# Taking two chunks through one half of the feed-forward features, then the other, in the first batch

## The chip, the cores and the metric

The kernel runs on one core of one Trainium2 chip. The metric is device time in microseconds (us) of one execution. A core has five engines with a queue of their own each: TensorE (PE) for matrix products, VectorE (DVE), ScalarE (ACT) and GpSimd (POOL) for elementwise work, and SyncE (SP), which here only issues transfers (DMA). They wait for one another by semaphores.

## The reference

```python
x: (8, 3008, 256) float32
X = np.fft.fft(np.fft.fft(x, axis=1), axis=2).real     # FNet mixing
x = X.reshape(8 * 3008, 256)
gate = 1 / (1 + np.exp(-(x @ w_gate)))                 # w_gate, w_val: (256, 1536)
out = (gate * (x @ w_val)) @ w_out                     # w_out: (1536, 256)
```

The three weights come as float64, and the kernel decodes them to float32 itself.

## The kernel before, in words

**Mixing.** A batch is folded by its symmetries (`fold_ops`), and its transform along the sequence is a set of matrix products with tables of cosines and sines (`seq_group`, `half`). Their results are evacuated by `places` into rows `pk` (cosines), `qk` (sines) and `ek` (the features' Nyquist row) of 1506 elements. For batch 0 the cosine products come first, in two halves as x arrives, then the sine products; `load_table` loads the tables.

**Weights.** The transform along the features is not done on x but on the weights: `merge` multiplies a gate or value weight block by a small table on TensorE (tile name `ps`), and ScalarE copies the result to `G1` and `G2`; two small transfers spread G2's first row to `ge`. A weight goes through the engines as a job: `weight_load` (a 512 KB transfer on SP), `weight_parts` (two ScalarE steps, L259 and L260), `weight_join` (three VectorE steps, L269, L270 and L272, then one on GpSimd, L274), and `weight_use`, which is the merge for gate and value blocks. `jobs` is the list of the 18 jobs, six blocks each of gate, value and output weights. An output weight block feeds `forms`: 11 sums (L315) and four ScalarE copies for each group of three feature tiles, in two parts, on GpSimd for groups 0 and 1 and on VectorE for 2 and 3.

**Feed-forward.** 1505 positions (mirrored, they make all 3008) are cut into six chunks of up to 252. The 1536 features are 12 tiles of 128, and the main loop has one iteration i for each batch, chunk and feature tile: 8 x 6 x 12 = 576. In an iteration TensorE does

- `front_a(i)`: two products with `pk` (gate and value), into a PSUM bank of `pf`
- a merge, where `use` holds one for this iteration
- `back`: a third (five products, tile names `po0` to `po4`) of the output products of the group of three feature tiles that ended two iterations earlier
- `front_b(i)`: two products with `qk`, onto the same bank of `pf`

Between them a copy `ae` of the bank is taken (on VectorE by L521 for i below 12, with the term of `ek` added; from 12 on by ScalarE, L518, on a bank that ScalarE has seeded with that term, L504). `gate_a(i-1)` and `gate_b(i-1)` then make both halves of h: VectorE forms z and two products, ScalarE two sigmoids, and GpSimd adds up the sums `sf` (L560) that the output products need (a bilinear scheme with 15 products in place of more). Then come the iteration's jobs: `pre` holds the rounds of parts and join, `use` the uses, and `parts_` the waiting parts of `forms`.

The output products of a chunk accumulate over its four groups in five PSUM banks. In the last group each bank is evacuated to a tile `c` (L584, ScalarE and VectorE in turn); `finish` puts the chunk's 20 sums of `c`, its transposes and its stores on the list `later`, from which each iteration takes two or three.

**Order.** All queues are strictly in the order in which the program is written (`manual_schedule`); nothing is rescheduled. Pools give buffers in turn: three PSUM banks for `pf` and `ps`, five for `po`; two tiles `c`; one `os`, which is `ek` of batch 0 before it serves for the stores. The staging of jobs 0 to 9 borrows tiles that the loop uses later (`home`), that of the later ones borrows the tile of x (three places for raw data), so they are loaded once the sine products of batch 0 have read x. The lines that place the jobs are

```python
for then, js in zip(evacuate, ((2, 3, 4), (5,), (), (), (6, 7), (8,))):
    weight_round(*js)
    then()()
```

that is, the rounds of jobs 2 to 8 between the six evacuations of batch 0's transform, and, in the loop, the round of job j (from 9) at iteration j - 9; the merges of block c at iterations 2c - 3 (gate) and 2c - 2 (value).

Of the kernel before, what the change touches and what calls it, by code (L numbers as in the profile page):

```python
# [75 lines left out]
def kernel(  # L76
# [122 lines left out]

    jobs = [(w, c - (w == 2)) for c in range(NPR + 1) for w in range(3)
            if (c if w == 2 else c < NPR)]
    RAW, WS = {}, {}
    shared = {}
    KEEP = 10
# [94 lines left out]
    def forms(g):  # L301

        w = [WO[f // 2].rearrange("p f (a h j) -> p f h a j", h=2, j=TB)[:, f % 2]
             for f in range(3 * g, 3 * g + 3)]
        f = wf[:, g].rearrange("p m (a j) -> p m a j", j=TB)
        engine = nc.gpsimd if g < 2 else nc.vector

        def block(i):
            return w[i // 2][:, i % 2] if i < 6 else f[:, i - 6]

        def some(lo, hi):
            for i, (a, sign) in enumerate(W_COPIES if lo == 0 else ()):
                nc.scalar.mul(f[:, len(W_SUMS) + i], block(a), float(sign))
            for i, (a, b, op) in list(enumerate(W_SUMS))[lo:hi]:
                engine.tensor_tensor(f[:, i], block(a), block(b), op=(ALU.subtract, ALU.add)[op])  # L315
        return [lambda lo=lo: some(lo, lo + 6) for lo in range(0, len(W_SUMS), 6)]
# [160 lines left out]

    chunks = [(k0, min(CH, -(-(NK - k0) // 3) * 3)) for k0 in range(0, NK, CH)]
    assert NK <= chunks[-1][0] + chunks[-1][1] <= NK + 1 and NFT == 12
    groups = [(b, c, g) for b in range(B) for c in range(len(chunks)) for g in range(NG)]  # L480
    H, SF, EK = {}, {}, {}

    def cut(i):
        b, c, _ = groups[i // 3]
        k0, n = chunks[c]
        f = i % NFT
        return PQE[b], slice(k0, k0 + n), n, f, slice(f * P, (f + 1) * P)

    def e_rows(i):

        b, c, _ = groups[i // 3]
        k0, n = chunks[c]
        EK[i // NFT] = ekp.tile([P, CH], F32, name="ek", tag="ek")[:, 0:n]
        nc.sync.dma_start(out=EK[i // NFT], in_=ed[b : b + 1, k0 : k0 + n].to_broadcast([P, n]))

    PF, AP, Z = {}, {}, {}

    def seed(i):


        _, _, n, f, _ = cut(i)
        PF[i] = bank("pf").rearrange("p (g n) -> p g n", g=2)[:, :, 0:n]
        for g in range(2 if i >= NFT else 0):
            nc.scalar.activation(PF[i][:, g], EK[i // NFT], AF.Copy, scale=ge[:, g, f : f + 1])  # L504

    def front_a(i):
        (pk, *_), ks, _, _, fs = cut(i)
# [59 lines left out]
    def back(p, part):  # L567

        b, c, g = groups[p]
        n = chunks[c][1]  # L570
        R = 2 * n // 3
        last = p == len(groups) - 1
        if part == 0 and g == 0:
            PO[:] = [pso.tile([P, 2 * WC], F32, name=f"po{t}", tag=f"po{t}") for t in range(NB)]
        for at_, (hb, wb) in list(enumerate(PRODUCTS))[part * 5 : part * 5 + 5]:
            t, j = divmod(PLACE[at_], 3)
            mm(PO[t][:, j * R : (j + 1) * R], wf[:, g, wb], block(p, hb), g == 0 and at_ % 3 == 0,
               g == NG - 1)
            if g == NG - 1 and at_ % 3 == 2:
                if t == 0:  # L580
                    C[0] = cp.tile([P, 10 * WC], F32, name="c", tag="c")
                    nc.gpsimd.memset(C[0][:, 15 * R : 15 * R + 40], 0.0)
                if not (last and t == NB - 1):
                    (nc.vector.tensor_copy if t % 2 else nc.scalar.copy)(  # L584
                        C[0][:, 3 * t * R : 3 * (t + 1) * R], PO[t][:, 0 : 3 * R])
        if part == 2:
            del H[p], SF[p]
            if g == NG - 1:
                finish(b, c, last)

    def finish(b, c, last):
        k0, n = chunks[c]
        R = 2 * n // 3
        more = k0 + n > NK
        nb = -(-n // TB)
        t = C.pop(0)
# [12 lines left out]

        def flip(s, h):  # L610
            if not os_:
                os_.append(op.tile([P, NK + 1], F32, name="os", tag="os")[:, 0 : 4 * WC].rearrange(
                    "p (s b h j) -> p s b h j", s=2, h=2, j=TB))
            c0 = OUT[h] * R + (n + more if s else 0)
            nc.vector.transpose(os_[0][:, s, 0:nb, h, :], t[:, c0 : c0 + nb * TB])

        def store(s):
            m, r0 = (min(n, M - k0), b * S + k0) if s == 0 else (
                n - (k0 == 0) - more, b * S + S - k0 - n + 1 + more)
            full = m // TB  # L620
            for a in range(4):
                ps = slice(a * TB, (a + 1) * TB)
                cs = slice(a * 2 * TB, (a + 1) * 2 * TB)
                queues[a % len(queues)].dma_start(
                    out=out[r0 : r0 + full * TB, cs].rearrange("(b t) d -> t b d", t=TB),
                    in_=os_[0][ps, s, 0:full].rearrange("p b h j -> p b (h j)"))
                if m > full * TB:
                    queues[a % len(queues)].dma_start(out=out[r0 + full * TB : r0 + m, cs],
                                      in_=os_[0][a * TB : a * TB + m - full * TB, s, full].rearrange(
                                          "p h j -> p (h j)"))  # L630

        def add(f):
# [21 lines left out]
        weight_load(j)  # L654
    load_x(0)
    load_table(0, NQ // 2)
    for j in range(2, 6):
        weight_load(j)
    load_table(1, NQ)
    for j in range(6, KEEP):  # L660
        weight_load(j)

    def weight_round(*js):
# [18 lines left out]
    for sums, _, _ in sin:  # L682
        sums(*range(NQ))
    evacuate = [then for _, then, _ in cos + sin]
    for then, js in zip(evacuate, ((2, 3, 4), (5,), (), (), (6, 7), (8,))):
        weight_round(*js)
        then()()
    nc.scalar.dma_start(out=ed[0:1], in_=PQE[0][2][0:1])
    nc.vector.tensor_copy(PQE[0][1][0:1, 0:CH], PQE[0][2][0:1, 0:CH])
    for j in range(KEEP, KEEP + 3):  # L690
        weight_load(j)
    weight_use(2)
# [4 lines left out]
    def at(i, *fs):  # L697
        side.setdefault(i, []).extend(fs)

    pre, use = {}, {}
    for j in range(9, len(jobs)):
        pre.setdefault(j - 9, []).append(lambda j=j: weight_round(j))
        if KEEP <= j < len(jobs) - 3:
            at(j - 9, lambda j=j: weight_load(j + 3))
    for j in range(3, len(jobs)):
        w, c = jobs[j]
        i = (0, 1, 4, 7, 9, 10)[c] if w == 2 else 2 * c - 3 + w
        use.setdefault(i, []).append(lambda j=j: weight_use(j))  # L710


# [2 lines left out]
    calm = lambda lo: (i for i in range(lo, count) if 3 <= i % i0 <= 7)  # L715
    for i, f in enumerate(mirror_x(1)):
        at(i0 - 3 + i // 2, f)
    at(i0 + 2, lambda: load_x(1))
    for b in range(1, B):
        at(i0 + 2 + b, lambda b=b: e_load(b))  # L720
    for i, f in enumerate(mirror_tables()):
# [1 line left out]
    at(3 * i0, e_fold)  # L723
    at(3 * i0 + 4, lambda: e_sums()())
    at(3 * i0 + 6, table_again)
    for i in range(i0, count, i0):
        at(i - 8, lambda i=i: e_rows(i))

    for b in range(B - 1):
# [1 line left out]
        g0 = s0 + 3 * i0 + 4 if b else 5 * i0 + 4  # L731


        slots = [i for i in range(s0 - 2 * i0 if b > 1 else s0 if b else 2 * i0, g0) if i % i0 < 4]

        def folds(slots, b=b):
            ops = fold_ops(b + 1, 2)
# [11 lines left out]
    for i in range(count):  # L749
        front_a(i)  # L750
        if i < NFT:
            part(i)
        if i:
            gate_a(i - 1)
        if i >= NFT:
            part(i)
        if i0 <= i + 1 < count:
            seed(i + 1)
        if i:
            gate_b(i - 1)  # L760
        todo = pre.pop(i, []) + use.pop(i, [])
        for f in [parts_.pop(0)] + todo if parts_ else todo + [lambda: parts_ and parts_.pop(0)()]:
            f()
        if i >= 5:
            back((i - 5) // 3, (i - 5) % 3)
        front_b(i)
        for f in later[0 : 2 + i % 2]:
            f()
        del later[0 : 2 + i % 2]
        for f in side.pop(i, []):  # L770
            f()
    gate_a(count - 1)
# [54 lines left out]
```

## Time and profile before

| what | value |
|---|---|
| median of 3 runs | 1982.71 us (1982.51 to 1985.28) |
| the profiled execution | 1985.11 us, its span 1983.2 us |
| TensorE busy | 1936.4 us, 98% of the span |
| VectorE, ScalarE, GpSimd busy | 1488.3, 1338.3, 1624.8 us |
| TensorE busy from 0 to 50 us | 32.70 us |
| TensorE busy from 50 to 130 us | 68.25 us |
| TensorE busy from 200 to 1900 us | 1696.71 us |
| first line of the loop on TensorE, second product of i = 0 | starts at 54.77 us |

All times in the profile count from the start of the span; the execution's own time is 1.9 us longer than the span. A row of the timeline gives the start, the length, the engine, the line, the operation, and the tiles written and read; in brackets stands how long the engine had been idle before it and what it waited for. Several instructions of one kind in a row are drawn together (xN). Two TensorE instructions in a row make one product here, so a product of `pf` for gate and value shows as x4, a merge as x8 and a third of the output products as x10. Lines named L127 are all TensorE's, since one helper issues every product.

### The profile page before, as it was taken

To read this page: it belongs to the slowest core of one execution; us is meant where nothing else is said; L and a number is where in the kernel's file an instruction comes from. 1 tells how busy PE (TensorE), PEld (TensorE's weight loads), DVE (VectorE), ACT (ScalarE), POOL (GpSimd) and SP (SyncE) were. 2 spreads that over 40 slices of the span, in tenths; PEclk is the share of its full clock that TensorE was granted. 3 is DMA by queue.
4 is the path that set the end of the run, shared out by engine and by line. 5 is a ranking of instruction groups with operands and counts; after the bars stand their busy time and mean duration, and the time that the engine had idled before them with its cause. 6 is when DMAs were issued, how large, how long until landed. Compare 5 with 4: busy or idle time off the path is not lost.

```text
span 1983.2 us, 34391 instructions
## 1 busy us (share of the span) xinstructions
PE 1936.4 (98%) x11232; PEld 1790.2 (90%) x11232; DVE 1488.3 (75%) x3179; ACT 1338.3 (67%) x3102; POOL 1624.8 (82%) x2857
## 2 busy tenths in 40 slices
PE   6899999999999999999999999999999999999997
PEld 4689889998999899998999989999899989999996
DVE  7788777886787677786778867787678777777776
ACT  3467667675777667775777757777577766777774
POOL 3879898997889878997889868998688886777775
PEclk8999999999999999999999999999999999999999
DMA  8353423212112120222013121221210110011001
GB/s 266 88 132 85 124 50 104 51 22 78 18 46 54 19 77 14 54 50 77 15 21 78 20 77 20 45 54 20 77 22 14 18 23 14 14 18 23 14 16 30
DMA packets 171444, 101.41 MB, mean 51 GB/s; under 512 B 133890, under 2 KB 163204, under 8 KB 168588
## 3 DMA queue, kind: packets, MB, share of 16 engines
q1 hardware_dynamic: 169294, 98.64, 20.3%
q8 instruction: 90, 1.47, 0.3%
q10 hardware_dynamic: 1940, 0.56, 0.1%
q14 instruction: 88, 0.72, 0.1%
q0 software_dynamic: 32, 0.00, 0.0%
HBM read 74.45 MB, written 50.18 MB: 63 GB/s over the span
## 4 chain that ended last, share of the span: by engine, by line
PE 94%; DMA 2%; DVE 2%; POOL 1%; ACT 1%; issue 0%; SPq 0%; ACTq 0%; DVEq 0%; POOLq 0%
PE pf L127 48%; PE po L127 41%; PE ev L127 4%; DMA ge<-G 1%; DMA st<-in_stab_dram 1%; PE od L127 1%; PE ps L127 0%; DVE wf L315 0%; DMA wx<-in_moe_w_val_dram 0%; DVE ae L521 0%; POOL sf L560 0%; POOL wf L315 0%; DVE z L539 0%; DMA raw<-in_moe_w_gate_dram 0%; DMA wx<-in_moe_w_gate_dram 0%
## 5 line engine op out<-in xcount | busy, mean ns | idle before, releaser
L560 POOL TENSOR_TENSOR sf<-h 128x168 f32<-128x168 f32 (+1 forms) x960 | 550.8, 592 | 233.1 <-DVE h L556 233.0
L560 POOL TENSOR_TENSOR sf<-h,sf 128x168 f32<-128x168 f32 (+1 forms) x1152 | 646.1, 581 | 54.2 <-DVE h L556 54.2
L127 PE MATMUL pf<-qk,G 128*128 128x252 f32 (+1 forms) x2304 | 582.7, 376 | 3.8 <-DVE ae L521 1.9
L127 PE MATMUL pf<-pk,G 128*128 128x252 f32 (+1 forms) x2304 | 583.0, 376 | 0.0
L556 DVE TENSOR_TENSOR h<-z 128x252 f32<-128x252 f32 (+1 forms) x576 | 293.7, 510 | 377.0 <-ACT z L555 376.4
L504 ACT ACTIVATE pf<-ek,ge 128x252 f32<-128x252 f32 (+1 forms) x1128 | 531.4, 471 | 18.4
L127 PE MATMUL po<-sf,wf 128*128 128x168 f32 (+1 forms) x3072 | 530.4, 306 | 0.0
L518 ACT ACTIVATE ae<-pf 128x504 f32<-128x504 f32 (+1 forms) x564 | 332.6, 590 | 240.1 <-PE pf L127 239.3
L127 PEld LDWEIGHTS pf<-pk,G 128*128 128x128 f32 x2304 | 436.3, 190 | 53.1 <-issue 2.3
L127 PEld LDWEIGHTS po<-sf,wf 128*128 128x128 f32 x3072 | 473.3, 190 | 8.4
L127 PE MATMUL po<-h,wf 128*128 128x168 f32 (+1 forms) x2688 | 475.9, 306 | 2.1 <-ACT a L471 1.6
L607 DVE TENSOR_TENSOR c<-c 128x168 f32<-128x168 f32 (+1 forms) x950 | 467.1, 514 | 8.5
L127 PEld LDWEIGHTS po<-h,wf 128*128 128x128 f32 x2688 | 427.5, 190 | 19.2 <-ACT a L471 2.0
L127 PEld LDWEIGHTS pf<-qk,G 128*128 128x128 f32 x2304 | 409.9, 190 | 30.7 <-DVE ae L521 2.9
L542 DVE TENSOR_TENSOR z<-ae,pf 128x504 f32<-128x504 f32 (+1 forms) x564 | 372.4, 660 | 19.1 <-ACT h L537 18.8
L537 ACT ACTIVATE h<-pf 128x252 f32<-128x252 f32 (+1 forms) x576 | 218.7, 380 | 172.3 <-PE pf L127 160.2
L555 ACT ACTIVATE z<-z 128x252 f32<-128x252 f32 (+1 forms) x576 | 230.8, 401 | 76.7 <-DVE z L542 46.5
L554 DVE TENSOR_TENSOR h<-h,pf 128x252 f32<-128x252 f32 (+1 forms) x576 | 231.7, 402 | 0.0
L560 POOL TENSOR_TENSOR sf<-sf 128x168 f32<-128x168 f32 (+1 forms) x192 | 114.3, 595 | 15.1
L127 PE MATMUL ev<-st,x 63*128 63x376 f32 (+4 forms) x372 | 99.0, 418 | 8.8 <-DVE x L338 6.0
L560 POOL TENSOR_TENSOR sf<-sf,h 128x168 f32<-128x168 f32 (+1 forms) x192 | 107.5, 560 | 0.0
L127 PEld LDWEIGHTS ev<-st,x 63*128 63x128 f32 (+1 forms) x372 | 66.8, 188 | 37.0 <-issue 7.3
(115 smaller groups left out, 876.5 us busy)
## 6 DMA issues: line engine op xcount, KB each, us to landing
x<-xr SPq DMA_DIRECT2D x14, 1536.0 KB
out_dram<-os SPq DMA_DIRECT2D x380, 56.0 KB
xr<-in_xf_dram SPq DMA_DIRECT2D x14, 768.0 KB
xr<-in_xf_dram SPq DMA_DIRECT2D x35, 256.0 KB
ek<-ed SPq DMA_DIRECT2D x39, 126.0 KB
out_dram<-os SPq DMA_DIRECT2D x288, 7.0 KB
x<-in_xf_dram SPq DMA_DIRECT2D x2, 1512.0 KB
tr<-in_stab_dram SPq DMA_DIRECT2D x2, 1129.5 KB
```

Source lines behind the costliest of these rows:

```text
L127: nc.tensor.matmul(o, l, r, start=start, stop=stop, skip_group_check=True)
L504: nc.scalar.activation(PF[i][:, g], EK[i // NFT], AF.Copy, scale=ge[:, g, f : f + 1])
L518: nc.scalar.activation(AP[i], PF[i], AF.Copy, scale=2.0)
L537: nc.scalar.activation(H[p][:, fh, 0:n], PF[i][:, 0], AF.Sigmoid)
L542: nc.vector.tensor_tensor(z[:, :, ::-1], AP.pop(i), PF[i], op=ALU.subtract)
L554: nc.vector.tensor_tensor(h[:, fh, 0:n], h[:, fh, 0:n], PF.pop(i)[:, 1], op=ALU.mult)
L555: nc.scalar.activation(z[:, 0], z[:, 0], AF.Sigmoid)
L556: nc.vector.tensor_tensor(h[:, fh, n:], z[:, 0], z[:, 1], op=ALU.mult)
L560: nc.gpsimd.tensor_tensor(block(p, dst), block(p, a), block(p, b), op=(ALU.subtract, ALU.add)[op])
L607: engine.tensor_tensor(t[:, dst * R : (dst + 1) * R], *v, op=(ALU.subtract, ALU.add)[op])
```

## The change

Chunks 0 and 1 of batch 0 are taken by halves of the features: chunk 0 with feature tiles 0 to 5 (iterations 0 to 5), chunk 1 with the same tiles (6 to 11), chunk 0 with tiles 6 to 11 (12 to 17), chunk 1 with those (18 to 23). From iteration 24 on the order is as before. The output products of each half accumulate on their own: the first half's banks are copied to `c`, the second half's are added to it by VectorE. Both chunks hold a tile `c` until they are finished, so C is kept by chunk.

So the weight blocks of the second half of the features are first used at iteration 12, not 6. Their jobs are put later in the list, and rounds and uses get new places; the rounds of jobs 2 to 6, not 2 to 8, stand between the evacuations. The forms of group 1 go from GpSimd to VectorE. Row 0 of `qk`, which carries `ek` for iterations below 12, does so for two chunks and is then set to zero; for iterations 12 to 23 ScalarE seeds the bank from `ek` itself. The sine table is loaded ahead of jobs 4 and 5. Batch 1's x is loaded at iteration 20, not 14, and its folds start at 26, not 24. While more than 24 steps are waiting in `later`, three are taken in every iteration.

```diff
-    jobs = [(w, c - (w == 2)) for c in range(NPR + 1) for w in range(3)
-            if (c if w == 2 else c < NPR)]
+    jobs = [(0, 0), (1, 0), (0, 1), (1, 1), (2, 0), (0, 2), (1, 2), (2, 1), (2, 2)]
+    jobs += [(w, c) for c in range(3, NPR) for w in range(2)] + [(2, c) for c in range(3, NPR)]
...
-        engine = nc.gpsimd if g < 2 else nc.vector
+        engine = nc.vector if g else nc.gpsimd
...
-    groups = [(b, c, g) for b in range(B) for c in range(len(chunks)) for g in range(NG)]
+    twice = [(0, 0), (0, 1)]
+    groups = [(*bc, g) for gs in (range(NG // 2), range(NG // 2, NG)) for bc in twice for g in gs]
+    groups += [(b, c, g) for b in range(B) for c in range(len(chunks)) for g in range(NG)
+               if (b, c) not in twice]
...
+        ek = pqe[2][:, ks] if groups[i // 3][:2] in twice else EK[groups[i // 3][:2]]
         PF[i] = bank("pf").rearrange("p (g n) -> p g n", g=2)[:, :, 0:n]
         for g in range(2 if i >= NFT else 0):
-            nc.scalar.activation(PF[i][:, g], EK[i // NFT], AF.Copy, scale=ge[:, g, f : f + 1])
+            nc.scalar.activation(PF[i][:, g], ek, AF.Copy, scale=ge[:, g, f : f + 1])
...
-        if part == 0 and g == 0:
+        halves = (b, c) in twice
+        g0, g1 = (g // 2 * 2, g // 2 * 2 + 1) if halves else (0, NG - 1)
+        if part == 0 and g == g0:
...
-                if not (last and t == NB - 1):
-                    (nc.vector.tensor_copy if t % 2 else nc.scalar.copy)(
-                        C[0][:, 3 * t * R : 3 * (t + 1) * R], PO[t][:, 0 : 3 * R])
+                dst, src = C[b, c][:, 3 * t * R : 3 * (t + 1) * R], PO[t][:, 0 : 3 * R]
+                if g0 == NG // 2:
+                    nc.vector.tensor_tensor(dst, dst, src, op=ALU.add)
+                elif not (last and t == NB - 1):
+                    (nc.vector.tensor_copy if t % 2 else nc.scalar.copy)(dst, src)
...
-    for j in range(2, 6):
+    for j in range(2, 4):
         weight_load(j)
     load_table(1, NQ)
-    for j in range(6, KEEP):
+    for j in range(4, KEEP):
         weight_load(j)
...
-    for then, js in zip(evacuate, ((2, 3, 4), (5,), (), (), (6, 7), (8,))):
+    for then, js in zip(evacuate, ((2,), (3,), (), (), (4, 5), (6,))):
...
-    nc.vector.tensor_copy(PQE[0][1][0:1, 0:CH], PQE[0][2][0:1, 0:CH])
+    nc.vector.tensor_copy(PQE[0][1][0:1, 0 : 2 * CH], PQE[0][2][0:1, 0 : 2 * CH])
...
-    for j in range(9, len(jobs)):
-        pre.setdefault(j - 9, []).append(lambda j=j: weight_round(j))
+    for j, i in enumerate((0, 1, 2, 4, 6, 7, 8, 10, 12, 13, 15), 7):
+        pre.setdefault(i, []).append(lambda j=j: weight_round(j))
         if KEEP <= j < len(jobs) - 3:
-            at(j - 9, lambda j=j: weight_load(j + 3))
-    for j in range(3, len(jobs)):
-        w, c = jobs[j]
-        i = (0, 1, 4, 7, 9, 10)[c] if w == 2 else 2 * c - 3 + w
+            at(i, lambda j=j: weight_load(j + 3))
+    for j, i in enumerate((0, 1, 1, 2, 1, 5, 4, 5, 7, 8, 10, 12, 14, 14, 17), 3):
         use.setdefault(i, []).append(lambda j=j: weight_use(j))
...
-    at(i0 + 2, lambda: load_x(1))
+    at(i0 + 8, lambda: load_x(1))
+    at(i0 - 1, lambda: nc.vector.memset(PQE[0][1][0:1, 0 : 2 * CH], 0.0))
...
-        slots = [i for i in range(s0 - 2 * i0 if b > 1 else s0 if b else 2 * i0, g0) if i % i0 < 4]
+        slots = [i for i in range(s0 - 2 * i0 if b > 1 else s0 if b else 2 * i0 + 2, g0) if i % i0 < 4]
...
-        for f in later[0 : 2 + i % 2]:
+        n = 3 if len(later) > 24 else 2 + i % 2
+        for f in later[0:n]:
             f()
```

The prediction speaks of the main loop's iterations as tiles (tile i is iteration i), and counts jobs in the new list unless it says otherwise; jobs 0 to 7 of the old list are the same as in the new one.

More of the change, by code (lines that the diff above doesn't have):

```diff
@@ L198, in table_again @@
             nc.sync.dma_start(out=ST[0][:, t, N3:, NE:], in_=tr[:, t, N3:, NE:])
-    jobs = [(w, c - (w == 2)) for c in range(NPR + 1) for w in range(3)
-            if (c if w == 2 else c < NPR)]
+    jobs = [(0, 0), (1, 0), (0, 1), (1, 1), (2, 0), (0, 2), (1, 2), (2, 1), (2, 2)]
+    jobs += [(w, c) for c in range(3, NPR) for w in range(2)] + [(2, c) for c in range(3, NPR)]
+    assert NPR == 6 and NG == 4
     RAW, WS = {}, {}
@@ L479 @@
     assert NK <= chunks[-1][0] + chunks[-1][1] <= NK + 1 and NFT == 12
-    groups = [(b, c, g) for b in range(B) for c in range(len(chunks)) for g in range(NG)]
+    twice = [(0, 0), (0, 1)]
+    groups = [(*bc, g) for gs in (range(NG // 2), range(NG // 2, NG)) for bc in twice for g in gs]
+    groups += [(b, c, g) for b in range(B) for c in range(len(chunks)) for g in range(NG)
+               if (b, c) not in twice]
+    assert chunks[0][1] == chunks[1][1] == CH
     H, SF, EK = {}, {}, {}
     def cut(i):
-        b, c, _ = groups[i // 3]
+        b, c, g = groups[i // 3]
         k0, n = chunks[c]
-        f = i % NFT
+        f = 3 * g + i % 3
         return PQE[b], slice(k0, k0 + n), n, f, slice(f * P, (f + 1) * P)
@@ L492, in e_rows @@
         k0, n = chunks[c]
-        EK[i // NFT] = ekp.tile([P, CH], F32, name="ek", tag="ek")[:, 0:n]
-        nc.sync.dma_start(out=EK[i // NFT], in_=ed[b : b + 1, k0 : k0 + n].to_broadcast([P, n]))
+        EK[b, c] = ekp.tile([P, CH], F32, name="ek", tag="ek")[:, 0:n]
+        nc.sync.dma_start(out=EK[b, c], in_=ed[b : b + 1, k0 : k0 + n].to_broadcast([P, n]))
     PF, AP, Z = {}, {}, {}
     def seed(i):
-        _, _, n, f, _ = cut(i)
+        pqe, ks, n, f, _ = cut(i)
+        ek = pqe[2][:, ks] if groups[i // 3][:2] in twice else EK[groups[i // 3][:2]]
         PF[i] = bank("pf").rearrange("p (g n) -> p g n", g=2)[:, :, 0:n]
         for g in range(2 if i >= NFT else 0):
-            nc.scalar.activation(PF[i][:, g], EK[i // NFT], AF.Copy, scale=ge[:, g, f : f + 1])
+            nc.scalar.activation(PF[i][:, g], ek, AF.Copy, scale=ge[:, g, f : f + 1])
     def front_a(i):
@@ L576, in back @@
             t, j = divmod(PLACE[at_], 3)
[L577 to L582, printed above, removed]
-                if not (last and t == NB - 1):
-                    (nc.vector.tensor_copy if t % 2 else nc.scalar.copy)(
-                        C[0][:, 3 * t * R : 3 * (t + 1) * R], PO[t][:, 0 : 3 * R])
+            mm(PO[t][:, j * R : (j + 1) * R], wf[:, g, wb], block(p, hb), g == g0 and at_ % 3 == 0,
+               g == g1)
+            if g == g1 and at_ % 3 == 2:
+                if t == 0 and g0 != NG // 2:
+                    C[b, c] = cp.tile([P, 10 * WC], F32, name="c", tag="c")
+                    nc.gpsimd.memset(C[b, c][:, 15 * R : 15 * R + 40], 0.0)
+                dst, src = C[b, c][:, 3 * t * R : 3 * (t + 1) * R], PO[t][:, 0 : 3 * R]
[3 more added lines that the diff above has]
+                    (nc.vector.tensor_copy if t % 2 else nc.scalar.copy)(dst, src)
         if part == 2:
@@ L595, in finish @@
         nb = -(-n // TB)
-        t = C.pop(0)
+        t = C.pop((b, c))
         queues = (nc.sync, nc.scalar) if last else (nc.sync,)
@@ L725 @@
     at(3 * i0 + 6, table_again)
-    for i in range(i0, count, i0):
+    for i in range(2 * i0, count, i0):
         at(i - 8, lambda i=i: e_rows(i))
@@ L766 @@
         front_b(i)
-        for f in later[0 : 2 + i % 2]:
+        n = 3 if len(later) > 24 else 2 + i % 2
+        for f in later[0:n]:
             f()
-        del later[0 : 2 + i % 2]
+        del later[0:n]
         for f in side.pop(i, []):
```

## The prediction

> **What bounds the kernel now.** I read the page's engine shares and its 40 slices first, then busy time by stretches of 10 us, TensorE's waits, and the timelines of TensorE, GpSimd and SyncE.
>
> ```profile
> PE 1936.4 (98%) x11232; PEld 1790.2 (90%) x11232; DVE 1488.3 (75%) x3179; ACT 1338.3 (67%) x3102; POOL 1624.8 (82%) x2857
> ...
> PE   6899999999999999999999999999999999999997
> ```
>
> TensorE sets the time: only the first two slices (49.6 us each) and the last show a gap, and between 200 and 1900 us it is busy 1696.7 of 1700. What can be won lies in the first 130 us. TensorE's waits between 50 and 128 us:
>
> ```profile
> engine line waited for: us in total, times, longest us
> PE ps L127 <- POOL wx L274: 7.3, 2, 6.1
> PE pf L127 <- DVE ae L521: 1.9, 2, 1.4
> PE ps L127 <- ACT G L296: 1.3, 3, 0.6
> PE ps L127 <- POOL sf L560: 0.6, 1, 0.6
> PE po L127 <- DVE wf L315: 0.4, 1, 0.4
> ```
>
> The merges (ps) stand for weights whose last step is on GpSimd. TensorE's timeline shows where:
>
> ```profile
> 41.11 3.51 PE L127 MATMUL ev<-st,x 126*128 126x377 f32 x6 [2.79 <-DMA st<-in_stab_dram]
> ...
> 50.47 1.89 PE L127 MATMUL ps<-raw,dt 128*128 128x256 f32 x8
> ...
> 54.77 1.01 PE L127 MATMUL pf<-qk,G 128*128 128x252 f32 x4
> ...
> 91.86 3.78 PE L127 MATMUL ps<-wx,dt 128*128 128x256 f32 x8 [6.08 <-POOL wx L274]
> ```
>
> The first line is a wait for the sine table. The third is the second product of tile 0, which I call b(0); b(i) is the same for tile i. From start to start a product takes 0.85, a merge 1.73, a third of an output group (po) 1.42; so a tile costs 2 x 0.85 + 1.42 = 3.13. From 50.47 to b(15) at 126.94 are 76.5 us, and their 10 merges, 31 products and 11 thirds make 59.3: **17.2 us are lost** there, 11.7 of them idle, the rest mostly a slow clock behind gaps. GpSimd's timeline says why:
>
> ```profile
> 62.31 1.06 POOL L315 TENSOR_TENSOR wf<-wf,wc 128x128 f32<-128x128 f32 x2
> ...
> 65.80 2.21 POOL L560 TENSOR_TENSOR sf<-h 128x168 f32<-128x168 f32 x4
> ...
> 72.53 1.46 POOL L274 TENSOR_TENSOR wx<-wx 128x512 int32<-128x512 int32 x1
> ```
>
> It works through forms of the output weights, sums of h and joins without a pause from 61 to 99 us. The join at 72.53 had been left by VectorE at 69.9.
>
> **The Trainium skill.** "TensorE: Matmul & The Clock Gate", Part 1: after an idle window of about 3.4 us the clock falls to half, and about as long a busy one restores it. The trace agrees in size (3.78 for eight matmuls against 1.89 behind the 6.08 gap), but a gap of 2.79 did it too: 3.51 for six against 2.06. "PSUM — Partial Sum Buffer", Engine vs sequencer instructions: the queues of ScalarE, VectorE and GpSimd are strict FIFO; the late join above agrees. "GPSIMD Engine Reference", Key points: GpSimd shares its SBUF interfaces with VectorE; the form sums on VectorE took 0.24 each at 106.45 and 0.53 at 106.97, with GpSimd busy. "DMA: Bandwidth & Descriptors", Queues, rings and completion order: a copy is split over up to 16 rings, each consumed in order; the weight load issued 0.7 us after the sines was awaited until 42.08, the sines until 40.98.
>
> **Part 1, sines sooner.**
>
> ```profile
> 19.99 0.37 SPq L252 DMA_DIRECT2D wf<-in_moe_w_out_dram  x1
> 21.93 0.37 SPq L252 DMA_DIRECT2D raw<-in_moe_w_gate_dram  x1
> 25.30 0.34 SPq L188 DMA_DIRECT2D st<-in_stab_dram  x1
> ```
>
> The sines take the first of these slots, and two loads of 0.52 MB go behind them. Up to the sines' end 11.1 MB were moved in about 39.5 us; 10.0 MB give 1.5 + 39.5 x 10.0/11.1 = 37.1. If the later loads take the share they had before, 38.9. The cosines end at 38.3. So the wait of 2.79 goes, and with it the slow clock behind it (9.36 us for the four sine groups, against 4 x 1.90). Gain 2.79 + 1.76 = **4.5 us** (3 if the table lands at 38.9 and the clock stays; 0 if it lands as before). Next late are the loads pushed back: joins 4 and 5 then end about 43.5 on VectorE, the sines' evacuation at 44.4, still before the merge of job 2 wants its bank at 45.9. The longer row copy (504 elements; 252 took 0.27, so 0.3 to 0.55) ends at about 47.6, and b(0) comes at 45.9 + 4.3 = 50.2: covered by merges and a product. Two joins move from before the loop into it; part 2 counts them.
>
> **Part 2, the loop's weights.** Counted from b(0). Tiles 0 to 2 have the same joins, merges and forms as before (jobs 7, 8, 9 in the places of 9, 10, 11), so b(3) is at 11.1 (before 11.5; no merge at tile 3). Now the merge of job 9 stands at tile 4. GpSimd reaches that join as before, behind 3.5 us of forms, seven sums (4.0 to 4.5) and 2.2 of forms: done at 18.6, while TensorE stands there at 12.8. That is **a new wait of 5.8 us**, with about 2.1 of slow clock behind it; before, TensorE had two merges and a tile to do meanwhile. On the other side the second forms (11 x about 0.5 = 5.5) leave GpSimd, so its long queue, which gave the 6.08 wait, is gone. They cost VectorE 11 x 0.47 = 5.1 (rows of L315) in tiles 5 and 6, ahead of the join of job 11, whose merge comes one tile later: VectorE has it at 34 to 35.8, GpSimd at 35.5 to 37.1, TensorE waits from 32: 3.5 to 5, again with a slow clock. b(7) comes out between 38.7 (second forms at 0.24, fast clock) and 42.7; I take **40.7, against 42.5** before. Then three merges are left, not one: 2 x 3.13 + 3 x 4.85 = 20.8 to b(12), against 19.8. From b(12) to b(20), 25.0 at full pace, come the last three joins and both late forms on VectorE. In the trace of before a VectorE queue about 3 us late at 118 to 122 cost TensorE 0.3. I take 1.0 (0 to 4). b(20) is then at 87.5, before 87.8: **the loop is even**, gain 0.3.
>
> **Part 3, the halves.** TensorE's products stay as many. Each of two chunks evacuates five banks twice: ten more sums of a bank and its copy on VectorE, not shown before; nearest is L542, 128x504 with one PSUM operand, 0.66: 6.6 us, less 4 copies of 0.67 kept as they were. They lie in tiles 20 to 28 beside 25 us of TensorE. VectorE's tile is about 1.6 plus two or three sums of C at 0.51; slack 0.3 on average, some 2 us behind at tile 28, and the slack of a tile covers it: 0.2 (0 to 3). Twelve tiles are seeded by ScalarE from the ek row block, as twelve were from its copy (L504, 0.47 each): nothing, and one 126 KB broadcast less. The memset of row 0 (between 0.06 and 0.5) waits for b(11) as VectorE's next step does anyway; b(12) is a merge and a third later: nothing. If that cover were gone, 0.5. The next x (3 MB, ten us at 310 GB/s) is asked for at tile 20, not 14, behind the seven small e loads on SP, and its first fold is at tile 26: 18 us for 10. On SP, loads 13 to 17 and the ge transfers stand behind one another, but ge of tiles 6 to 11 is first read at tile 11.
>
> **Sum.** -4.5 - 0.3 + 0.2 = -4.6. Against the profiled execution (1985.11; span 1983.2) that is 1980.5; it ran 2.4 above the median, and against the median of 1982.71 it is **1978.1**.
>
> **Rivals.** (A, the forecast) as above, -1.5 to -8. (B) The loop's waits go: halved demand leaves TensorE bound by VectorE's joins only (4.0 a tile where a product pair and a merge take 3.4), 3.5 at tiles 1 to 4 and 2 around tile 6, so 5.5 of 17.2 stay: -4.5 - 11.7 = -16.2, 1966.5; half of it would be 1974. For it speaks GpSimd's relief; against it, the join of job 9 is still third behind first forms and sums. (C) The sines don't come sooner, since the table shares the rings with what follows, and the rest is even: 1981 to 1984. Against: 5.3 us earlier issue. (D, slower) VectorE's queue at tiles 12 to 28. Its work at the slow rows: 8 x 1.6, three joins at 2.35, 22 forms at 0.465, copies and memset 1.6 make 31.7 in the 26.8 us to tile 19; three sums of C at each tile (3.1 of 3.13) then keep the queue from draining while the adds come. ScalarE waits for z from VectorE, and TensorE's next product for ScalarE. It decides once the queue is more than 3 us late at tile 20; price 4 + 3, with b(7) at its late end 2 more: -4.5 + 9 = +4.5, 1987.
>
> **Chances.** A 0.57, B 0.13, C 0.11, D 0.19. A measurement here tells about 0.2% (4 us). Faster by more: 0.42 of A and all of B, 0.55 (two slow clocks are in A's sum, and each may be missing). Within: 0.15 of A, 0.09 of C, 0.02 of D, 0.26. Slower: 0.02 of C, 0.17 of D, 0.19. The range, 1970 to 1986.5, holds A and C, the weaker half of B and the start of D; A's own is 1974.5 to 1981.
>
> **What would show it.** Right: no wait of TensorE on the sine table, the four sine groups in 7.6 us, b(0) near 50; a wait of the merge at tile 4 on a join by GpSimd of 5 to 6 us with eight matmuls in 3.7; a second such wait at tile 7 of 3 to 5; from tile 28 on TensorE busy without a gap. Wrong: a merge at tile 4 that doesn't wait (B), a sine wait still there (C), gaps at po or pf behind VectorE or ScalarE between tiles 13 and 30 (D).

## The result, and the profile after

The changed kernel is **slower**: 1997.77 us median (1996.57 to 1998.01, four runs) against 1983.57 (1982.51 to 1985.28) for the kernel before in the same comparison. The ratio is 1.0065, 95% interval 1.0053 to 1.0077, about 13 us. The forecast was 1978.1 (1970 to 1986.5): wrong in sign and outside its range. The profiled execution took 1998.01 us, its span 1996.0 against 1983.2; this 12.8 is what the traces have to explain.

The engine shares of the page after, and TensorE's slices:

```profile
PE 1940.1 (97%) x11232; PEld 1794.0 (90%) x11232; DVE 1499.9 (75%) x3201; ACT 1336.0 (67%) x3102; POOL 1616.5 (81%) x2846
...
PE   6799899999999999999999999999999999999997
```

TensorE does the same 11232 matmuls and is busy 3.7 us longer (some run at a slow clock); the rest of the 12.8 is idle. A slice is 49.9 us: the second has fallen from 8 to 7, and the fifth, from 200 to 250 us, from 9 to 8. So a part of the loss lies later than the prediction looked. The second product of a tile, the prediction's b(i), dates it (us from the start of each span; the last column is the difference that the prediction's steps give):

| second product of | before | after | after - before | predicted |
|---|---|---|---|---|
| tile 0 | 54.77 | 52.16 | -2.6 | -4.6 |
| tile 7 | 97.31 | 95.45 | -1.9 | -6.4 |
| tile 12 | 117.14 | 117.28 | +0.1 | -5.4 |
| tile 20 | 142.56 | 146.89 | +4.3 | -4.9 |
| tile 40 | 205.06 | 211.78 | +6.7 | -4.7 |
| tile 41 | 214.13 | 226.89 | **+12.8** | -4.7 |

Behind tile 41 the difference stays between 12.8 and 13.3. TensorE's timeline of the changed kernel, the lines that answer to those of before and every gap above 1 us from 40 to 230 us:

```profile
40.19 2.14 PE L127 MATMUL ev<-st,x 126*128 126x377 f32 x6 [0.30 <-DMA st<-in_stab_dram]
...
47.85 1.89 PE L127 MATMUL ps<-raw,dt 128*128 128x256 f32 x8
...
52.16 1.01 PE L127 MATMUL pf<-qk,G 128*128 128x252 f32 x4
...
63.59 1.40 PE L127 MATMUL pf<-qk,G 128*128 128x252 f32 x4 [2.16 <-DVE ae L529]
...
70.27 3.78 PE L127 MATMUL ps<-wf,dt 128*128 128x256 f32 x8 [3.59 <-POOL wf L275]
...
89.49 3.78 PE L127 MATMUL ps<-wx,dt 128*128 128x256 f32 x8 [5.28 <-POOL wx L275]
...
131.63 1.12 PE L127 MATMUL pf<-qk,G 128*128 128x252 f32 x4 [1.68 <-ACT ae L526]
...
136.96 1.12 PE L127 MATMUL pf<-qk,G 128*128 128x252 f32 x4 [1.42 <-ACT ae L526]
...
180.38 1.12 PE L127 MATMUL pf<-qk,G 128*128 128x252 f32 x4 [1.63 <-ACT ae L526]
...
223.93 3.17 PE L127 MATMUL po<-h,wf 128*128 128x168 f32 x10 [7.97 <-ACT a L472]
```

The wait on the sine table is down from 2.79 to 0.30. In place of one long wait on a join there are two (70.27 and 89.49, each with a merge at half speed behind it), and tile 3 waits 2.16 for VectorE's `ae`. Tiles 16, 17 and 30 wait for ScalarE's copy `ae`, which the kernel before didn't do there. And between tiles 40 and 41 TensorE stands 8 us for a copy at L472.

TensorE's waits between 50 and 128 us (total, times, longest), GpSimd's timeline with the two joins that TensorE waited for, and VectorE's ahead of the second of them:

```profile
engine line waited for: us in total, times, longest us
PE ps L127 <- POOL wx L275: 5.3, 1, 5.3
PE ps L127 <- POOL wf L275: 3.6, 1, 3.6
PE pf L127 <- DVE ae L529: 2.2, 1, 2.2
PE ps L127 <- DVE h L562: 0.8, 1, 0.8
PE ps L127 <- ACT G L297: 0.3, 1, 0.3
```

```profile
67.11 1.68 POOL L316 TENSOR_TENSOR wf<-wf 128x128 f32<-128x128 f32 x4
68.75 1.47 POOL L275 TENSOR_TENSOR wf<-wf 128x512 int32<-128x512 int32 x1
...
88.15 1.28 POOL L275 TENSOR_TENSOR wx<-wx 128x512 int32<-128x512 int32 x1 [0.68 <-DVE wx L273]
```

```profile
85.09 0.62 DVE L316 TENSOR_TENSOR wf<-wc 128x128 f32<-128x128 f32 x1
85.64 0.76 DVE L270 TENSOR_SCALAR wx<-wx 128x512 f32<-128x512 f32 x1
...
87.11 0.91 DVE L273 SCALAR_TENSOR_TENSOR wx<-wx 128x512 int32<-128x512 int32 x1
```

TensorE's waits in this window are no shorter than before (12.2 us in these five rows against 11.5 in the five of before); they fall on other tiles. The join of job 9 still stands behind the first forms on GpSimd; that of job 11 now comes late from VectorE, which takes it up right behind the second forms (L316).

**What holds that copy.** L472 is in `e_sums`, which runs once, at iteration 40, and makes a row tile `er` for the other batches. All engines of the changed kernel there:

```profile
215.61 0.43 DVE L627 STREAM_TRANSPOSE os<-c 128x256 f32<-128x256 f32 x1
...
220.56 0.43 SPq L640 DMA_DIRECT2D out_dram<-os  x1
...
222.25 0.06 DVE L464 MEMSET er<- 7x1 f32 x1 [5.40 <-DMA out_dram<-os]
...
223.41 0.47 ACT L472 COPY a<-pe 7x376 f32<-7x376 f32 x1 [7.47 <-DVE er L422]
...
223.93 3.17 PE L127 MATMUL po<-h,wf 128*128 128x168 f32 x10 [7.97 <-ACT a L472]
```

`er` is allocated from the pool with the one output buffer (`er = op.tile(..., tag="os")`). It can't be written until the last store of chunk 1 has read `os`. In the kernel before, chunks 0 and 1 ended at iterations 16 and 28, and the list `later` was empty after iteration 37; `er` then found the buffer free. All engines of the kernel before:

```profile
204.78 0.42 SPq L628 DMA_DIRECT2D out_dram<-os  x1
...
208.36 0.06 DVE L463 MEMSET er<- 7x1 f32 x1
...
210.75 1.69 PE L127 MATMUL po<-h,wf 128*128 128x168 f32 x10 [1.61 <-ACT a L471]
```

With the halves they end at 22 and 28. At iteration 28 the last 9 steps of chunk 0 still stand ahead of the 24 of chunk 1, so the last step of chunk 1 falls to iteration 40 itself: its transpose comes at 215.61, right ahead of `er`. VectorE waits 5.40 for the stores, ScalarE's copy for VectorE, and the ten products for the PSUM bank that this copy frees.

**What holds ae at tiles 16 and 17.** VectorE's timeline of the changed kernel:

```profile
131.12 0.62 DVE L316 TENSOR_TENSOR wf<-wx 128x128 f32<-128x128 f32 x1
131.66 0.76 DVE L270 TENSOR_SCALAR wx<-wx 128x512 f32<-128x512 f32 x1
132.46 0.65 DVE L271 TENSOR_SCALAR wx<-wx 128x512 int32<-128x512 int32 x1
133.14 0.91 DVE L273 SCALAR_TENSOR_TENSOR wx<-wx 128x512 int32<-128x512 int32 x1
133.97 0.67 DVE L597 COPY c<-po 128x504 f32<-128x504 f32 x1
134.57 0.66 DVE L550 TENSOR_TENSOR z<-ae,pf 128x504 f32<-128x504 f32 x1
```

ScalarE's:

```profile
135.26 0.41 ACT L563 ACTIVATE z<-z 128x252 f32<-128x252 f32 x1 [2.82 <-DVE z L550]
```

The end of the third forms, the join of job 17 and a bank copy stand ahead of z without a pause; ScalarE waits 2.82 for z, and its next `ae` is late for TensorE at 136.96 (tile 17). What held tile 16 is tested by e4 below.

### The profile page after: what moved, and what is told of

It is laid out like the page before. It is cut to its first block, busy times and chain, and to the rows that moved or that the text cites. A ratio compares the mean times of both kernels' runs of the same rounds, so it can differ in the third digit from the quotient of the medians.

```text
span 1996.0 us, 34376 instructions
## 1 busy us (share of the span) xinstructions
PE 1940.1 (97%) x11232; PEld 1794.0 (90%) x11232; DVE 1499.9 (75%) x3201; ACT 1336.0 (67%) x3102; POOL 1616.5 (81%) x2846
## 3 DMA queue, kind: packets, MB, share of 16 engines
q8 instruction: 90, 1.47, 0.3%
## 4 chain that ended last, share of the span: by engine, by line
PE 92%; DVE 3%; DMA 2%; ACT 1%; POOL 1%; SPq 1%; issue 0%; DVEq 0%; ACTq 0%
PE pf L127 47%; PE po L127 40%; PE ev L127 4%; DMA st<-in_stab_dram 2%; PE ps L127 1%; DVE wf L316 1%; DVE c L619 1%; PE od L127 1%; ACT z L563 0%; DVE h L564 0%; DVE z L550 0%; POOL wf L316 0%; SPq L640 0%; DVE ae L529 0%; SPq L636 0%
## 5 line engine op out<-in xcount | busy, mean ns | idle before, releaser
L550 DVE TENSOR_TENSOR z<-ae,pf 128x504 f32<-128x504 f32 (+1 forms) x564 | 372.6, 661 | 18.6 <-ACT h L545 18.4
L545 ACT ACTIVATE h<-pf 128x252 f32<-128x252 f32 (+1 forms) x576 | 217.9, 378 | 170.1 <-PE pf L127 158.9
L568 POOL TENSOR_TENSOR sf<-sf 128x168 f32<-128x168 f32 (+1 forms) x192 | 114.3, 596 | 15.1
```

Of the source, the lines that this page charges most:

```text
L545: nc.scalar.activation(H[p][:, fh, 0:n], PF[i][:, 0], AF.Sigmoid)
L550: nc.vector.tensor_tensor(z[:, :, ::-1], AP.pop(i), PF[i], op=ALU.subtract)
L568: nc.gpsimd.tensor_tensor(block(p, dst), block(p, a), block(p, b), op=(ALU.subtract, ALU.add)[op])
```

## The experiments

Each is set against the kernel before in runs on the same chip. Where a number of a tile is given, it is the start of its second product in the profiled execution. The changed kernel stands at ratio 1.0065.

### e1_own_er: the row tile in a place of its own

```diff
-        er = op.tile([P, NK + 1], F32, name="er", tag="os")[0:m]
+        er, _ = [pqp.tile([P, NK + 1], F32, name="er", tag="pk") for _ in range(2)]
+        er = er[0:m]
```

> The changed kernel with one edit: the row tile er of the sums at tile 40 gets a place of its own (a free rotation of pk) in place of the one output buffer os. Theory (the largest part of the loss is er waiting for the stores of chunk 1, which now end just before tile 40): 1997.8 - 6.0 = about 1991.8 us (1990.5 to 1993), the wait of 8 us ahead of the ten products at tile 40 is gone and the ten take 1.6 in place of 3.17 us. Rival (VectorE is behind by then and would hold ScalarE's copy anyway): within 1 us of the changed kernel, 1997 to 1998.

1993.16 us, ratio 1.0045 (1.0032 to 1.0057). From tile 40 to 41: 11.0 us, after 15.1, before 9.1. So the buffer costs 4.1, and 1.9 of the 6.0 that the theory gave it has another cause. Its trace, all engines:

```profile
215.15 0.43 DVE L628 STREAM_TRANSPOSE os<-c 128x256 f32<-128x256 f32 x1
...
215.50 0.87 DVE L620 TENSOR_TENSOR c<-c 128x168 f32<-128x168 f32 x2
...
216.31 0.53 DVE L419 TENSOR_TENSOR er<-a,pe 7x377 f32<-7x377 f32 x1
...
217.90 3.17 PE L127 MATMUL po<-h,wf 128*128 128x168 f32 x10 [2.40 <-ACT a L473]
```

The wait on the stores is gone; now three steps of `later` stand ahead of `er` on VectorE, TensorE waits 2.40, and the clock still falls (3.17 in place of 1.69).

### e3_later_merges: jobs 9 to 13 merged later

```diff
-    for j, i in enumerate((0, 1, 1, 2, 1, 5, 4, 5, 7, 8, 10, 12, 14, 14, 17), 3):
+    for j, i in enumerate((0, 1, 1, 2, 1, 5, 6, 7, 9, 10, 11, 12, 14, 14, 17), 3):
```

> The changed kernel with the merges of jobs 9, 10, 11, 12 and 13 at tiles 6, 7, 9, 10 and 11 in place of 4, 5, 7, 8 and 10; rounds and loads as they are. Theory (TensorE stands 3.6 and 5.3 us at the merges of jobs 9 and 11 and then runs at the slow clock; two tiles later their joins are done): the two waits go, tile 12 starts 3 to 8 us sooner, 1990 to 1995 us. Rival (VectorE and GpSimd are what the tiles 3 to 8 wait for; a merge moved only moves the wait): less than 1 us, 1997 to 1998.

1994.19 us, ratio 1.0049 (1.0036 to 1.0061): 3.2 us below the changed kernel by the ratios, 5.4 by the spans. Against the changed kernel tile 7 starts 10.3 sooner, tile 12 5.0 and tile 20 5.0. The two long waits are gone. Of the 5.3 that are lost again between tiles 7 and 12, 1.7 is one merge that now lies there and not ahead of tile 7; most of the rest is new waits, one for VectorE's `ae` and one at the moved merge of job 13. TensorE's timeline:

```profile
89.21 1.12 PE L127 MATMUL pf<-qk,G 128*128 128x252 f32 x4 [0.51 <-DVE ae L529]
...
103.15 1.97 PE L127 MATMUL ps<-wx,dt 128*128 128x256 f32 x8 [2.27 <-POOL sf L568]
```

### e4_forms2_gpsimd: the third forms on GpSimd

```diff
-        engine = nc.vector if g else nc.gpsimd
+        engine = nc.vector if g % 2 else nc.gpsimd
```

> The changed kernel with the weight sums forms(2) on GpSimd in place of VectorE (eleven additions). Theory (tiles 14 to 20 lose 4.2 us because VectorE's queue holds z and the copies ae behind forms, joins and bank copies): tile 20 starts 2 to 4 us sooner, 1994 to 1996 us. Rival (GpSimd's feature sums then come late and the products wait for sf): 1998 to 2003.

2001.57 us, ratio 1.0083 (1.0069 to 1.0096), as the rival had it. Its tile 12 starts at 117.28, as in the changed kernel. Tile 16 then starts at 130.00 in place of 131.63, with no wait for `ae`: these forms on VectorE were what made tile 16 late. But tile 18 starts at 143.94 in place of 140.21. TensorE's timeline:

```profile
136.88 2.05 PE L127 MATMUL po<-h,wf 128*128 128x168 f32 x6 [4.32 <-POOL wf L316]
```

GpSimd works on these forms, with its sums of h between them, from 128.4 to 137.2, later than the products need them. At this place the work is on the path on either engine.

### e2_sines_only and e6_sines_rounds: part 1 alone

Both are the kernel before with the sine table loaded ahead of jobs 4 and 5. They differ in where the rounds go that no longer fit ahead of it:

```diff
 e2_sines_only
-    for then, js in zip(evacuate, ((2, 3, 4), (5,), (), (), (6, 7), (8,))):
+    for then, js in zip(evacuate, ((2, 3), (), (), (4,), (5, 6, 7), (8,))):
 e6_sines_rounds
+    for then, js in zip(evacuate, ((2,), (3,), (), (), (4, 5), (6,))):
...
-    for j in range(9, len(jobs)):
-        pre.setdefault(j - 9, []).append(lambda j=j: weight_round(j))
+    for j in range(7, len(jobs)):
+        pre.setdefault(max(j - 8, 0), []).append(lambda j=j: weight_round(j))
...
```

> The kernel before with the sines' load moved ahead of the loads of jobs 4 and 5 (and the rounds of jobs 2 to 7 shifted to later evacuations to fit); groups, jobs and halves as before. The prediction's part 1: 4.5 us less than before, about 1979. What the changed kernel's trace shows at its first tile: 2.6 less, about 1981. Rival (what is gained ahead of the loop is waited away at the first merges, whose joins are as late as before): no difference, 1983 to 1984.

e2: 1989.38 us, ratio 1.0025 (1.0016 to 1.0034): slower, which neither the theory nor the rival had. The table comes in time (first sine products at 39.54, no wait), but tile 0 starts at 58.28, since the joins of jobs 5, 6 and 7 stand on VectorE ahead of the first evacuation of `qk`, which starts at 50.70 (46.95 in the kernel before).

> The kernel before with the sines loaded ahead of jobs 4 and 5 and the rounds as in the changed kernel: job 2, then 3, then 4 and 5, then 6 at the evacuations, 7 and 8 at tile 0, and the rounds of jobs 9 to 17 one tile later; groups, jobs and merges as before. e2_sines_only started its first tile 3.5 us later than before, since three joins stood ahead of the sines' evacuation. Theory (the sines sooner are worth 2.6 to 3.6 us at the first tile once no join stands there, and the loop gives back a part because two joins now lie in tile 0): first tile at 51 to 52 us, the whole 1981 to 1984. Rival (the loop gives back more than the start gains): 1985 to 1988.

e6: 1991.91 us, ratio 1.0040 (1.0027 to 1.0052): slower still, beyond the rival too. Tile 0 starts at 52.11, as hoped; tile 12 at 124.42, 7.3 later than before. TensorE's timeline says where the gain went:

```profile
77.82 3.78 PE L127 MATMUL ps<-wx,dt 128*128 128x256 f32 x8 [5.89 <-POOL wx L274]
...
94.98 3.78 PE L127 MATMUL ps<-wx,dt 128*128 128x256 f32 x8 [4.80 <-POOL wx L274]
...
116.38 1.65 PE L127 MATMUL pf<-qk,G 128*128 128x252 f32 x4 [4.54 <-DVE ae L521]
```

Jobs 7 and 8 are decoded in tile 0 and all later ones a tile later, with their merges where they were. How much of this is the two extra joins and how much the later rounds isn't told apart. What it shows: the sines' gain isn't one by itself, since it takes VectorE's time in the opening, and joins put off into the loop are paid for there.

### e5_no_adds: the halves without their additions

```diff
                 if g0 == NG // 2:
-                    nc.vector.tensor_tensor(dst, dst, src, op=ALU.add)
+                    pass
```

> The changed kernel with the ten additions of banks to the copies left out: the output of the first two chunks then holds one half of the features alone. The prediction priced these ten at 0.2 us (0 to 3). Theory (they make VectorE late at tiles 20 to 31, where the changed kernel loses 2.4 us against the kernel before): 1.6 to 2.4 us less than the changed kernel, about 1995.5, with tile 30 no later than tile 20 was. Rival (the c sums at three a tile are what makes VectorE late there): less than 0.5 us, about 1997.5.

1996.46 us, ratio 1.0063 (1.0049 to 1.0077). By medians that is within the error of the changed kernel. The two traces say more: tile 12 to 20 takes 29.6 us in both, so the additions have no part there; tile 20 to 40 takes 63.1 in place of 64.9, and the gap at tile 30 is gone. The additions cost 1.8 us of TensorE's time in tiles 20 to 31. At tile 40 this kernel stands 7.97 us for `er` all the same.

### e7_er_merges and e8_spread: together, and spread

e7 has the edits of e1 and e3. e8 moves rounds and uses on top of it:

```diff
-    for j, i in enumerate((0, 1, 2, 4, 6, 7, 8, 10, 12, 13, 15), 7):
+    for j, i in enumerate((0, 1, 2, 5, 7, 8, 9, 10, 11, 12, 14), 7):
...
-    for j, i in enumerate((0, 1, 1, 2, 1, 5, 6, 7, 9, 10, 11, 12, 14, 14, 17), 3):
+    for j, i in enumerate((0, 1, 1, 2, 1, 6, 6, 7, 9, 10, 11, 12, 13, 13, 16), 3):
```

> The changed kernel with both edits of e1_own_er (er in a place of its own) and e3_later_merges. Theory (the wait for the one output buffer and the early merges are separate losses, so they add): 4.6 us of e1 and 3.6 of e3 below 1997.8, about 1989.6 to 1990; tile 41 about 3 us later than in the kernel before. Rival (both end in the same VectorE queue, so they overlap): 1992 or more.

1991.26 us, ratio 1.0038 (1.0026 to 1.0051): 5.4 below the changed kernel by the ratios, where e1 and e3 alone gave 4.0 and 3.2. That lies between the two expectations. The buffer's 4.1 us come out in full (tile 40 to 41 takes 11.0, in e3 15.1); what is missing is at the merge of job 13, which stood 2.27 us as in e3 but then ran in 3.58 in place of 1.97, at the slow clock.

> e7_er_merges with the rounds of jobs 10 to 13 one tile later and those of 15 to 17 one tile sooner, the use of job 8 (which starts forms(1)) one tile later and the uses of jobs 15 to 17 one tile sooner. Theory (VectorE is full at tiles 3 to 8 and 14 to 20 and has idle stretches at tiles 10 to 13, so work moved there comes off the path): 2 to 5 us below e7, 1985 to 1988. Rival (no tile from 3 to 20 has room on VectorE): within 1 us of e7.

1988.40 us, ratio 1.0019 (1.0010 to 1.0027): 2.9 below e7 by the medians, 3.8 by the ratios, as the theory had it. Tile 12 to 20 takes 28.2, in e7 30.8. But tile 10 to 11 takes 11.35. All engines of e8:

```profile
102.27 0.41 DVE L563 TENSOR_TENSOR h<-h,pf 128x252 f32<-128x252 f32 x1
...
102.83 3.75 PE L127 MATMUL ps<-wx,dt 128*128 128x256 f32 x8 [3.71 <-POOL sf L569]
```

The trace names GpSimd, whose join of this job was done at 101.8; what ends 0.15 us ahead of the merge is VectorE's h, the last reader of the previous tile's `pf`. From iteration 11 on the next tile's bank is already seeded, so a merge needs the third of three banks and must wait for that h. The merges of jobs 13 and 14 in e3, e7 and e8 are of this kind, and that of job 14 in the changed kernel; the two long waits of the changed kernel (tiles 4 and 7) aren't.

### e9_all: the merge behind the products

```diff
+        if i >= i0 - 1:
+            back((i - 5) // 3, (i - 5) % 3)
         for f in [parts_.pop(0)] + todo if parts_ else todo + [lambda: parts_ and parts_.pop(0)()]:
             f()
-        if i >= 5:
+        if 5 <= i < i0 - 1:
             back((i - 5) // 3, (i - 5) % 3)
...
-        n = 3 if len(later) > 24 else 2 + i % 2
+        n = 0 if i == 3 * i0 + 4 else 2 + i % 2
```

> e8_spread with three edits: from tile 11 on the five products of a tile stand ahead of the tile's merge (in e8 the merge of job 13 at tile 11 stood 3.7 us, from 99.1 to 102.8, until VectorE's h had read the third bank, and then ran at the slow clock); the c sums are taken two and three a tile in turn as in the kernel before; and none at tile 40, so that the sums of er find VectorE free. Theory: 3 to 5 us at tile 11, about 1 at tile 30, up to 2 at tile 40, so 1982 to 1985, level with the kernel before or a little faster. Rival (what TensorE doesn't wait at tile 11 it waits at tiles 12 to 20 for VectorE): 1986 to 1988.

1983.14 us against 1984.51, ratio 0.9992 (0.9984 to 1.0000): level with the kernel before, or faster by a bit more than 1 us; the interval just reaches no change. Tile 10 to 12 takes 11.8 in place of 17.2, tile 40 to 41 9.3 in place of 11.0. With `er` in its own place and VectorE free at tile 40, all but 0.2 of the 6.0 is gone there, though this execution loses 1.7 at tile 42 behind it, at a slow clock (last section). TensorE's timeline:

```profile
207.56 1.69 PE L127 MATMUL po<-h,wf 128*128 128x168 f32 x10 [1.61 <-ACT a L473]
```

### e10_before_merges: the same cure on the kernel before

```diff
-        i = (0, 1, 4, 7, 9, 10)[c] if w == 2 else 2 * c - 3 + w
+        i = (0, 1, 4, 7, 9, 10)[c] if w == 2 else 2 * c - 3 + w + (c > 2)
```

> The kernel before with the merges of the feature pairs 3 to 5 one tile later (tiles 4 to 9 in place of 3 to 8); nothing else. Theory (the early merge is a loss that both kernels have: in the kernel before TensorE stood 6.08 us at tile 6 for the join of a pair and then ran a merge at 3.78 in place of 1.97 us): 3 to 7 us faster than before, 1977 to 1981. Rival (the tiles wait for VectorE and GpSimd whatever the merge does, and the wait moves to ae and sf): within 1 us of the kernel before.

1984.47 us against 1984.51, ratio 0.9999 (0.9990 to 1.0007): no difference, as the rival had it. From its tile 0 to 20 it took 85.4 us where the kernel before took 87.8, and the wait of 6.08 is gone; but 3.44 came back as a wait for `ae`, and 1.7 was lost at tile 42 (below).

### e11_third_copy and e12_before_third

Both take the wait out of `e_sums` that is left in the kernel before, e12 alone, e11 on top of e9 (with the merge of job 10 a tile later as well); `e2` is a free part of the tile of `er`:

```diff
+        nc.scalar.copy(e2[:, 0:NO], ps[at_(1, 1), 0:NO])
...
-            nc.scalar.copy(a[:, 0:NO], ps[at_(1, 1), 0:NO])
-            places(er, 1, False, e1[:, 0:NO], a[:, 0:NO])
+            places(er, 1, False, e1[:, 0:NO], e2[:, 0:NO])
```

> e9_all with two edits: the fourth piece of the sums at tile 40 is copied out of PSUM at once, into partitions 32 to 38 of er's own tile, in place of waiting for the buffer a until VectorE has read it; and the merge of job 10 at tile 8 in place of 7. Theory (in e9 TensorE stood 1.61 and 1.88 us at tile 40 and 41 for that copy and what follows it, the second then cost 1.7 at a slow clock, and 3.1 us plus 1.5 of slow clock at the merge of job 10): 2 to 5 us below e9 at tile 42, 0 to 3 at tile 8; 1978 to 1981. Rival (VectorE's er placements hold z and h at tile 41 whatever ScalarE copies, and the merge only moves its wait): within 1 us of e9, 1982.5 to 1984.

> The kernel before with the same copy alone: the fourth piece of the sums at tile 40 goes at once into partitions 32 to 38 of er's tile. Theory (the 1.61 and 1.68 us that TensorE stands at tiles 40 and 41 in the kernel before are ScalarE's wait for VectorE inside e_sums): 1.5 to 3 us faster than before, 1981.5 to 1983. Rival (VectorE holds z and h there whatever is copied): within 0.5 us of the kernel before.

e12: 1984.15 us against 1984.60, ratio 1.0000 (0.9991 to 1.0008); e11: 1983.29 us, ratio 0.9994 (0.9986 to 1.0002). Both rivals came true. In e12, all engines:

```profile
210.75 0.53 DVE L421 TENSOR_TENSOR er<-pe,a 7x376 f32<-7x376 f32 x1
...
211.43 1.66 PE L127 MATMUL po<-h,wf 128*128 128x168 f32 x10 [1.66 <-DVE er L421]
```

VectorE reads the same bank itself and ends at 211.28, when the copy would have ended too (210.70 in the kernel before, whose tile 40 starts 0.63 sooner). So the wait changes its name and keeps its length. In e11 tile 8 was 0.9 sooner and tile 12 1.4 later than in e9. No version here is faster than the kernel before by more than the error.

## Why the prediction was wrong

- **Part 1, the sines (predicted -4.5).** The mechanism held: the wait fell to 0.30 us and the four sine groups took 7.7. But the sum has the table landing too early: TensorE waited for it until 40.2, not 37.1 to 38.9, and the wait was short only because the cosine products, too, ended later (39.9; before 38.3). They started 1.1 us later (22.21 against 21.15) and took 0.5 longer, so the profiled pair shows -2.6. Nine traces with the new opening start tile 0 at 50.5 to 52.3, mean 51.6; three with the old one at 54.8 to 56.0, mean 55.4. So the gain is about 3.8, and the 2.6 is partly chance.
- **Part 2 up to tile 7 (predicted 40.7 from b(0), 38.7 to 42.7)** took 43.3. The joins came about when forecast: that of job 9 was done at 68.75 + 1.47, which is +18.1 (predicted 18.6), that of job 11 at +35.9 on VectorE (34 to 35.8) and at +37.3 on GpSimd (35.5 to 37.1), with TensorE standing from +32.0 (32). The waits were of other sizes. The first was 3.59, not 5.8, since the join was 0.5 sooner and TensorE came there 1.7 late itself: behind the wait of 2.16 at tile 3 its products ran at a slow clock (1.88 in place of 1.01 at 64.79), which the steps leave out. The second was 5.28 (3.5 to 5), and the merge and the third behind it cost 2.8 more than at full speed. Late joins and slow clocks added up, to more than the upper end allowed.
- **Part 2, tiles 7 to 12 (predicted 20.8)** took 21.8; the merge of job 14 at tile 12 waited 0.79 for its bank.
- **Part 2, tiles 12 to 20 (predicted 1.0 late, 0 to 4)** were 4.6 late. This term failed most within the steps that were worked out. It was sized from a VectorE queue that was 3 us late once in the kernel before; here forms, joins and bank copies follow one another, z comes late, and TensorE stands 1.68 and 1.42 us for `ae`. e4 shows that the forms hold tile 16, e8 that moving forms and joins together one tile sooner brings 2.6 us back (against e7). How much of the rest is the bank copies and how much the join wasn't tried.
- **Part 3, the additions (predicted 0.2, 0 to 3)** cost 1.8 by e5. "From tile 28 on TensorE busy without a gap" was wrong at tile 30, where it stood 1.63 us for `ae`. e9 with the c sums at two and three a tile has gaps of only 0.39 and 0.25 there.
- **The step that was missing**: `er` at tile 40, 6.0 us, nearly half of the loss. By e1 4.1 of it is the output buffer; the rest is steps of `later` ahead of `er` on VectorE, since e9, which takes none at tile 40, wins 1.7 of it. The prediction looked at chunks 0 and 1 up to tile 28, and left the later end of their sums and stores out of its sum. The diff doesn't touch `e_sums`; only the list of users of the tag `os` and the length of `later` at iteration 40 would have told.
- **Rival D** had the sign, the place (tiles 12 to 28) and nearly the price: it gave the loop +9, and tiles 0 to 40 lost 9.3. Its 9 with the measured start and the missing step makes -2.6 + 9 + 6.0 = 12.4 of the 12.8. Its sign, gaps behind ScalarE's `ae` between tiles 13 and 30, stands in the trace at tiles 16, 17 and 30. It deserved more than 0.19: its own sum of VectorE's work, 31.7 us in 26.8, was already in the text.

## What to carry to other kernels

When a change delays the end of some work, list every later user of each buffer which that work holds, in code that the diff doesn't touch too; a pool with one buffer makes neighbours in time out of steps that have nothing to do with one another. Work moved out of an opening is only free if the engine that takes it in the loop has room: here e6 lost 10 us between tiles 0 and 12 after gaining 2.7 ahead of them. And a wait taken away ahead of a loaded engine (e3, e10) comes back in smaller pieces; count what that engine still has to do before counting the wait as gain.

## What the runs showed of the hardware

- **The clock can fall behind gaps of about 2 us.** "TensorE: Matmul & The Clock Gate", Part 1, of the Trainium skill speaks of about 3.4 us of idle time. In e1 a gap of 2.40 was enough (ten products 3.17 in place of 1.69, the granted clock 0.52 from 217.9 to 221.1). In e10 two gaps of 1.62 and 1.85, with ten products (1.69) between them, slowed the next ones. TensorE's timeline of e10:

```profile
213.50 1.17 PE L127 MATMUL pf<-qk,G 128*128 128x252 f32 x4 [1.85 <-ACT ae L518]
...
214.47 1.93 PE L127 MATMUL pf<-pk,G 128*128 128x252 f32 x4
```

  The same product takes 1.04 in the kernel before, where the gaps are 1.61 and 1.68. It isn't a sharp bound: e11 had 1.64 and 1.88 and kept its clock, e9 with 1.61 and 1.88 lost it, 1.7 us of difference at tile 42. At tile 3 the changed kernel fell to a clock of 0.61 behind a gap of 2.16 (63.6 to 66.7), and e9 kept 1.00 behind a gap of the same length (63.2 to 66.1).
- **VectorE's sums of 128x128 differ by more than two.** In the changed kernel at 78 to 86 us the eleven second forms took 0.24 to 0.63 each. The short ones started while GpSimd stood idle, the long ones while it worked; no run here tests whether GpSimd is the cause.
